# A four-row lead load and an earlier weight at the front of a bandwidth-bound channel-attention kernel

## The chip, the cores and the metric

The kernel runs on one core of one Trainium2 chip. The metric is device time in microseconds (us) for one execution. "Before" and "changed" are the two kernels. TensorE multiplies matrices, VectorE and ScalarE work element by element. SyncE and ScalarE issue the transfers, each on a queue of its own; 16 DMA engines move the packets of both queues.

## The reference

The input `x` has 1 x 384 x 384 x 384 elements in bf16 (113.25 MB), and `w1d` is a single number. The mean of every channel over all pixels, times the weight, goes through a sigmoid. Every pixel is then multiplied by that gate.

```python
g = jnp.einsum("bhwc->bc", x) / (H * W)
s = sigmoid(g * w1d[0])          # kernel size 1: no neighbours
return x * s[:, None, None, :]
```

The gate depends on all of `x`, so an honest first reading would load everything before storing anything. The kernel avoids that with a guess that it checks.

## The kernel before: the parts that matter

Each of the 128 partitions holds rows of 384 channels. There are 1152 rows per partition: one small first tile of `FIRST = 8` rows, then 26 tiles of `TILE = 44` rows in `SLOTS = 6` slots of on-chip memory (SBUF). The kernel computes an early gate, `s_early`, from only `EARLY = 4` rows of the first tile, gates and stores all tiles with it, and sums everything on TensorE on the side. At the end it computes the true gate and compares the two in bf16. Only if they differ does it run a second pass, which did not happen here.

```python
FIRST, EARLY, TILE, SLOTS, BOTH = 8, 4, 44, 6, 4
# the front: what is loaded, in which order, on which queue
load(base, FIRST, 0)                                   # SyncE: 8 rows, 128 x 6144 B
for k in range(BOTH):                                  # tiles 0..3: one half on each queue
    load(slot(k), TILE, row0(k), ("sync", "scalar"))   # 128 x 16896 B each
    if k == 0:
        plan.dma("scalar", w_one[0:1, 0:1], w1d.unsqueeze(0), writes=["w_one"])
for k in range(BOTH, SLOTS):                           # tiles 4, 5: SyncE, 128 x 33792 B
    load(slot(k), TILE, row0(k))
weight()      # TensorE broadcasts the weight, VectorE scales it
sum_first()   # TensorE sums the 4 early rows
# ... add_banks (VectorE), then s_early = sigmoid(...) on ScalarE
plan.need("tensor", ["zeros"] + rows(base, FIRST))     # TensorE waits for all 8 rows
sum_others()  # rows 4..7 of the first tile, then tile 0, 1, ...
# ... cut
for k in range(n_tiles):
    if k >= SLOTS:
        put(slot(k), TILE, row0(k - SLOTS))  # VectorE gates in place, ScalarE issues the store
        load(slot(k), TILE, row0(k))         # SyncE waits for that store, then loads
# ... cut: at the end the last six tiles and the first tile are put, then the check
ahead("sync", nc.sync, 1)     # this many transfers are issued before the start barrier
ahead("scalar", nc.scalar, 1)
```

Every store is issued on ScalarE's queue, behind that queue's own loads. VectorE gates a tile in place, so it waits until TensorE has summed that tile. TensorE works in order: the weight, the early rows, the other rows of the first tile, tile 0, and so on.

## Time and profile before

| | before |
|---|---|
| device time, median of 3 runs | 529.17 us (529.02 to 529.28) |
| span of the profiled execution | 527.6 us |
| bytes moved | 226.5 MB, half read, half written |
| TensorE busy, VectorE busy | 46%, 46% |

These are lines of the page of the kernel before. The DMA line is the busy share of the 16 DMA engines in tenths over 40 slices of 13.2 us, and the GB/s line is what they moved. The last three lines are loads: queue, number, size, and median time from issue to landing.

```profile
span 527.6 us, 1093 instructions
...
DMA  9999999999999999999999999999999999999998
GB/s 384 430 429 410 428 438 436 425 446 418 443 425 441 436 425 446 418 443 420 446 433 428 443 420 443 420 446 433 428 443 420 441 423 443 436 425 446 416 443 358
...
HBM read 113.25 MB, written 113.25 MB: 429 GB/s over the span
...
arena<-in_x_dram ACTq DMA_DIRECT2D x4, 2112.0 KB, 26.0
arena<-in_x_dram SPq DMA_DIRECT2D x4, 2112.0 KB, 30.5
arena<-in_x_dram SPq DMA_DIRECT2D x1, 768.0 KB, 7.1
```

The DMA engines are at 90% or more in every slice but the last, so the 46% of the two compute engines says that neither of them limits the time.

These are lines of the timeline of the kernel before, at its front. The columns are start, duration, engine, line, operation, count, and in brackets the idle time before it and what ended it.

```profile
12.60 0.16 PE L337 MATMUL w_all<-w_one,ones 1*128 1x1 bf16 x1 [12.60 <-DMA w_one<-in_w1d_dram]
...
16.93 0.61 ACT L369 ACTIVATE s_early<-total,w_scaled 128x384 bf16<-128x384 f32 x1 [12.55 <-DVE total L311]
17.32 8.81 PE L238 MATMUL acc<-arena,ones 128*128 128x512 bf16 x33 [1.88 <-PEq L279]
26.24 17.83 DVE L202 TENSOR_TENSOR arena<-arena,s_early 128x16896 bf16<-128x16896 bf16 x2 [9.35 <-PE acc L238]
...
35.23 0.36 ACTq L109 DMA_DIRECT2D out_dram<-arena  x1
```

The weight's matmul waited 12.60 us for the weight's landing. `s_early` was made from 16.93 us on. TensorE started on tile 0 at 17.32, VectorE on its first gate at 26.24, and the first store was issued at 35.23 us.

These are windows of the kernel before. The last two columns are the DMA share and GB/s. A packet's bytes count where it starts, so short windows wobble and the share can pass 1.

```profile
core 0: us, PE busy (x) PEld busy (x) DVE busy (x) ACT busy (x) POOL busy (x), PEclk, DMA share, GB/s
1.00:2.50 1.50, 0.00 (x0) 0.00 (x0) 0.17 (x1) 0.00 (x0) 0.06 (x2) 1.00 0.94 325
...
8.00:38.00 30.00, 19.38 (x74) 0.21 (x2) 14.51 (x10) 0.61 (x1) 0.00 (x0) 0.99 1.00 427
38.00:46.00 8.00, 7.95 (x31) 0.00 (x0) 6.07 (x1) 0.00 (x0) 0.00 (x0) 0.82 1.02 382
...
70.00:500.00 430.00, 206.33 (x712) 0.00 (x0) 188.13 (x21) 0.00 (x0) 0.00 (x0) 0.72 1.00 433
500.00:527.00 27.00, 0.62 (x3) 0.00 (x0) 14.32 (x11) 0.61 (x1) 0.00 (x0) 0.60 0.96 411
```

Between 70 and 500 us the rate is 433 GB/s. It is clearly lower in three places only: at the front, between 38 and 46 us, and at the end. To account for every tenth of a microsecond I use one derived number, the **lag**: time since the start of the span minus the bytes moved so far divided by 433.3 GB/s, with each packet's bytes of the two queues spread over its duration. At the end of the span the lag is 527.56 us minus 226.496 MB (both queues, all packets) / 433.3 GB/s = 4.84 us. At this rate, that is the most that any reordering could win.

### The profile page before, as it was taken

Reading aid. Unit: us, or ns where it says so; the run is one execution under the profiler, and the core shown is the slowest. Engines: PE = TensorE matmul, PEld = TensorE weight load, DVE = VectorE, ACT = ScalarE, POOL = GpSimd, SP = SyncE. Lnnn points to the kernel's source line nnn. Section 1 sums busy time; section 2 is a strip of 40 time slices with the busy share of each in tenths; the row PEclk is TensorE's granted clock in tenths of the full one; section 3 lists DMA queues with packets and bytes.
Section 4 is the critical chain, followed back from the end, with each engine's and each line's share of the span. In section 5 each row is a group of like instructions: output and inputs, shape, how many; then the busy total and the mean of one; then the engine's idle time right before and its main releaser. Section 6 shows DMA issues by size and latency. Waiting matters only on the chain. (4 is left out here: it accounts for less than half of the span.)

```text
span 527.6 us, 1093 instructions
## 1 busy us (share of the span) xinstructions
PE 243.7 (46%) x851; PEld 0.2 (0%) x2; DVE 241.1 (46%) x45; ACT 2.7 (1%) x4; POOL 0.3 (0%) x6
## 2 busy tenths in 40 slices
PE   0876561652651651652742642642733733633700
PEld 0000000000000000000000000000000000000000
DVE  0298626326336336336246336246156156156190
ACT  1000000000000000000000000000000000000000
POOL 0000000000000000000000000000000000000000
PEclk9998867866767867866757867868757768768765
DMA  9999999999999999999999999999999999999998
GB/s 384 430 429 410 428 438 436 425 446 418 443 425 441 436 425 446 418 443 420 446 433 428 443 420 443 420 446 433 428 443 420 441 423 443 436 425 446 416 443 358
DMA packets 8357, 226.53 MB, mean 429 GB/s; under 512 B 930, under 2 KB 930, under 8 KB 1186
## 3 DMA queue, kind: packets, MB, share of 16 engines
q10 hardware_dynamic: 4466, 121.90, 53.6%
q1 hardware_dynamic: 3888, 104.60, 46.2%
q8 instruction: 1, 0.02, 0.0%
q14 instruction: 2, 0.02, 0.0%
HBM read 113.25 MB, written 113.25 MB: 429 GB/s over the span
## 5 line engine op out<-in xcount | busy, mean ns | idle before, releaser
L238 PE MATMUL acc<-arena,ones 128*128 128x512 bf16 x846 | 242.6, 453 | 244.3 <-PEq L279 242.7
L202 DVE TENSOR_TENSOR arena<-arena,s_early 128x16896 bf16<-128x16896 bf16 (+1 forms) x27 | 234.5, 8691 | 259.2 <-PE acc L238 259.2
L337 PE MATMUL w_all<-w_one,ones 1*128 1x1 bf16 x1 | 0.2, 158 | 12.6 <-DMA w_one<-in_w1d_dram 12.6
L346 DVE TENSOR_SCALAR w_scaled<-w_all 128x1 f32<-128x1 f32 x2 | 0.2, 154 | 11.6 <-PE w_all L337 11.6
L311 DVE TENSOR_TENSOR total<-total,acc 128x128 f32<-128x128 f32 (+2 forms) x11 | 4.5, 408 | 0.3
L393 ACT ACTIVATE arena<-total,w_scaled 128x384 bf16<-128x384 f32 x1 | 0.6, 615 | 495.7 <-DVE total L311 495.7
L331 ACT ACT_TABLE_LOAD x1 | 1.3, 1283 | 2.9 <-issue 2.9
L309 DVE COPY total<-acc 128x384 f32<-128x384 f32 x1 | 0.6, 558 | 1.2 <-PE acc L238 1.2
L401 DVE TENSOR_TENSOR total<-arena,s_early 128x384 f32<-128x384 uint16 x1 | 0.6, 559 | 0.7 <-ACT arena L393 0.7
L238 PE MATMUL acc<-zeros,ones 128*128 128x512 bf16 x3 | 0.8, 380 | 0.0
L369 ACT ACTIVATE s_early<-total,w_scaled 128x384 bf16<-128x384 f32 x1 | 0.6, 615 | 12.5 <-DVE total L311 12.5
L355 DVE MEMSET ones<- 128x128 bf16 x1 | 0.2, 165 | 1.0 <-PEq L522 1.0
L236 PE MATMUL acc<-arena,ones 128*128 128x512 bf16 x1 | 0.6, 607 | 0.0
L409 DVE TENSOR_REDUCE wrong<-total 128x1 f32<-128x384 f32 x1 | 0.6, 553 | 0.0
L331 ACT ACTIVATE warm<-warm 128x1 f32<-128x1 f32 x1 | 0.2, 203 | 0.0
L415 DVE CAST redo<-wrong 128x1 int32<-128x1 f32 x1 | 0.2, 153 | 0.0
L236 PEld LDWEIGHTS acc<-arena,ones 128*128 128x128 bf16 x1 | 0.1, 106 | 0.0
L337 PEld LDWEIGHTS w_all<-w_one,ones 1*128 1x128 bf16 x1 | 0.1, 100 | 12.6 <-issue 12.6
L522 POOL MEMSET const-bfloat16-1.0<- 128x1 bf16 x1 | 0.1, 101 | 0.0
L522 POOL MEMSET const-uint8-127<- 128x1 uint8 x1 | 0.1, 101 | 0.0
L354 POOL MEMSET zeros<- 128x2 bf16 x1 | 0.1, 99 | 0.0
L353 POOL MEMSET warm<- 128x1 f32 x1 | 0.1, 98 | 0.5 <-POOLq L522 0.5
(2 smaller groups left out, 0.2 us busy)
## 6 DMA issues: line engine op xcount, KB each, us to landing
out_dram<-arena ACTq DMA_DIRECT2D x26, 4224.0 KB, 52.7
arena<-in_x_dram SPq DMA_DIRECT2D x22, 4224.0 KB, 48.1
arena<-in_x_dram ACTq DMA_DIRECT2D x4, 2112.0 KB, 26.0
arena<-in_x_dram SPq DMA_DIRECT2D x4, 2112.0 KB, 30.5
arena<-in_x_dram SPq DMA_DIRECT2D x1, 768.0 KB, 7.1
out_dram<-arena ACTq DMA_DIRECT2D x1, 768.0 KB, 16.8
w_one<-in_w1d_dram ACTq DMA_DIRECT2D x1, 0.0 KB
```

Source lines behind the costliest of these rows:

```text
L202: return lambda e: e.tensor_tensor(to_v, v, s_b, ALU.mult)
L236: loaded.append(e.matmul(bank, weights, moving, start=start, stop=stop))
L238: return e.add_instruction(mybir.InstMatmult(name=nc.get_next_instruction_name(), engine=mybir.EngineType.PE, ins=[e.lower_ap(moving), e.l ...
L309: emit = lambda e, part=part, of=of: e.tensor_copy(part, of)
L311: emit = lambda e, part=part, of=of: e.tensor_tensor(part, part, of, ALU.add)
L331: lambda e: e.activation(warm[:, 1:2], warm[:, 0:1], ACT_F.Sigmoid),
L337: lambda e: e.matmul(w_all[:, 0:1], ones[0:1, :], w_one[0:1, 0:1], start=True, stop=True),
L346: lambda e, i=i, n=n: e.tensor_scalar_mul(w_scaled[:, i : i + 1], w_all[:, 0:1], 1.0 / float(P * n)),
L369: lambda e: e.activation(s_early[:], total[:], ACT_F.Sigmoid, scale=w_scaled[:, 0:1]),
L393: lambda e: e.activation(s_true, total[:], ACT_F.Sigmoid, scale=w_scaled[:, 1:2]),
L401: lambda e: e.tensor_tensor(total[:], s_true.bitcast(U16), s_early[:].bitcast(U16), ALU.not_equal),
L409: lambda e: e.reduce_max(wrong[:], total[:], axis=mybir.AxisListType.X),
```

## The change

The intent is to get the early gate sooner. Only the 4 rows that it needs lead SyncE's queue. The weight, which stood on ScalarE's queue behind one half of tile 0 (2.2 MB), follows them directly. The other 4 rows come behind the two halves of tile 0, two rows on each queue.

```diff
-    def load(place, n, r0, queues=("sync",)):
-        i = 0
-        for queue, m in zip(queues, split(n, -(-n // len(queues)))):
+    def load(place, n, r0, queues=("sync",), lo=0, hi=None):
+        i, hi = lo, hi or n
+        for queue, m in zip(queues, split(hi - lo, -(-(hi - lo) // len(queues)))):
 ...
-    load(base, FIRST, 0)
+    load(base, FIRST, 0, hi=EARLY)
+    plan.dma("sync", w_one[0:1, 0:1], w1d.unsqueeze(0), writes=["w_one"])
     for k in range(BOTH):
         load(slot(k), TILE, row0(k), ("sync", "scalar"))
         if k == 0:
-            plan.dma("scalar", w_one[0:1, 0:1], w1d.unsqueeze(0), writes=["w_one"])
+            load(base, FIRST, 0, ("sync", "scalar"), lo=EARLY)
 ...
-    ahead("sync", nc.sync, 1)
+    ahead("sync", nc.sync, 2)
```

More of the change, by code (lines that the diff above doesn't have):

```diff
@@ L463, in ahead @@
         block[barrier:barrier] = new
-    ahead("sync", nc.sync, 1)
+    ahead("sync", nc.sync, 2)
     ahead("scalar", nc.scalar, 1)
-    plan.emit("sync", nc.sync, heads["sync"] - 1)
+    plan.emit("sync", nc.sync, heads["sync"] - 2)
     plan.emit("scalar", nc.scalar, heads["scalar"] - 1)
```

## The prediction

> **What bounds the kernel now.** The page counts 226.5 MB in a span of 527.6 us, 429 GB/s on average, and a DMA share of at least 0.9 in 39 of 40 slices; TensorE and VectorE are busy 46% each. Summing the trace's packet records in half-microsecond stretches, the 16 DMA engines run at 430 to 435 GB/s from about 8 us to 525 us. The Trainium skill ("DMA: Bandwidth & Descriptors", "Where 436 GB/s comes from") gives 435 GB/s as the ceiling of the 16 ports; the trace's 433 agrees. At 433 GB/s the bytes alone take 523.1 us. Only 4.5 us are lost: the first packet starts at 1.05 us, the engines fill by 1.75 us and run at 375 to 425 GB/s until 6 us; a dip to half rate at 40.3 to 42.6 us (about 1 us lost); and an uneven end, 525.3 to 527.1 us.
>
> **What the change does.** SyncE's first load shrinks from 128 x 6144 B to 128 x 3072 B; the other 4 rows follow behind the two halves of tile 0 as 2 x 128 packets of 1536 B; the weight leaves ScalarE's queue, where it landed at 12.5 us behind a 2.1 MB half tile, and becomes SyncE's second transfer. Bytes are unchanged, 2 DMA issues are added (0.33 to 0.5 us each by the timeline), and SyncE issues two transfers before the start barrier, which may delay the other engines by 0.4 us.
>
> **The early chain gains.** The lead load landed at 7.1 us because each DMA engine alternates by packet between the two queues (same page, "Queues, rings and completion order"; in this trace 6144 B packets take turns with 16896 B ones). I expect it at 3.5 to 4.5 us with the weight close behind; s_early, ready at 17.5 us, comes at 8 to 10 us. Tile 0's second half, landed at 17.1 us, comes at 13 to 15. Its sum on TensorE starts at about 14 instead of 17.3 us, the first gate at about 23 instead of 26.2, the first store's issue at about 32 instead of 35.2.
>
> **None of it is on the critical path.** The loads of six tiles fill the DMA engines beyond 60 us, and the first store's packets (42.6 us) stand in ScalarE's queue behind its own four half-tile loads, not behind the gate. The end (last store issued at 510.7, DMA full to 525) is untouched.
>
> **A small cost at the front.** ScalarE's first packets come at 2.46 us. Until 3.3 us the old lead load covered their slow ramp with its backlog, 0.1 to 0.15 MB. With half the bytes that backlog is gone: 0.2 to 0.3 us of DMA time lost (estimate from those records), unless ScalarE's packets come earlier. Smaller packets (0.79 MB) cost under 0.1 us more.
>
> **Predicted:** 529.3 us, range 528.5 to 530.2. Faster by over 2%: 1%; within 2%: 98%; slower by over 2%: 1%.
>
> **Checks.** Lead load and weight landing under 5 us; s_early before 11 us; first gate near 23 us; first store packet still near 42 us; DMA rate between 2 and 3.5 us lower than before; 430 to 435 GB/s from 8 to 525 us, the dip apart; span within 1 us.
>
> **What would make it wrong.** The dip near 41 us may hang on the order of transfers and vanish or double (1 us either way). The new interleaving may leave the engines less even at the end, or a queue may run dry once the stores begin: up to 1 us.

## The result, and the profile after

| | before | changed |
|---|---|---|
| device time, median of 4 runs | 529.16 us (529.02 to 529.28) | 529.04 us (528.93 to 529.18) |
| ratio | | 0.9998, 95% interval 0.9981 to 1.0015 |
| span of the profiled execution | 527.6 us | 527.5 us |

A ratio is the mean time of one kernel's fast runs over that of the other's of the same rounds, so it is not quite the ratio of the medians quoted. The verdict, at a threshold of 2%, is "same".

The page of the changed kernel, lines as shown before:

```profile
span 527.5 us, 1096 instructions
...
DMA  9999999999999999999999999999999999999998
GB/s 369 437 428 424 443 418 448 415 448 423 438 438 423 448 413 451 420 441 431 431 446 415 451 418 443 425 436 446 415 448 420 441 425 436 448 415 448 416 443 353
...
HBM read 113.25 MB, written 113.25 MB: 429 GB/s over the span
...
arena<-in_x_dram ACTq DMA_DIRECT2D x4, 2112.0 KB, 25.8
arena<-in_x_dram SPq DMA_DIRECT2D x4, 2112.0 KB, 29.6
...
arena<-in_x_dram SPq DMA_DIRECT2D x1, 384.0 KB, 3.9
arena<-in_x_dram ACTq DMA_DIRECT2D x1, 192.0 KB, 13.0
arena<-in_x_dram SPq DMA_DIRECT2D x1, 192.0 KB, 15.3
```

The lead load lands 3.9 us after its issue instead of 7.1. The trailing rows are the last two lines, and SyncE's part of them takes 15.3 us.

The timeline of the changed kernel at its front:

```profile
4.86 0.16 PE L338 MATMUL w_all<-w_one,ones 1*128 1x1 bf16 x1 [4.86 <-DMA w_one<-in_w1d_dram]
...
9.18 0.61 ACT L371 ACTIVATE s_early<-total,w_scaled 128x384 bf16<-128x384 f32 x1 [4.41 <-DVE total L312]
16.97 9.91 PE L239 MATMUL acc<-arena,ones 128*128 128x512 bf16 x36 [10.56 <-DMA arena<-in_x_dram]
27.00 17.83 DVE L202 TENSOR_TENSOR arena<-arena,s_early 128x16896 bf16<-128x16896 bf16 x2 [17.85 <-PE acc L239]
...
35.99 0.36 ACTq L109 DMA_DIRECT2D out_dram<-arena  x1
```

The weight's matmul moved from 12.60 to 4.86 us and `s_early` from 16.93 to 9.18 us: the change does what it is meant to do. But TensorE's next work starts at 16.97 us, hardly earlier than before, and the first gate at 27.00 and the first store's issue at 35.99 us are both 0.76 us *later*. The next line is from the waits of the changed kernel (total, times, longest); before, no such wait of TensorE for a load of `x` appeared.

```profile
PE acc L239 <- DMA arena<-in_x_dram: 10.6, 1, 10.6
```

The idle time of TensorE ended with a load's landing. By the landing records, tile 0's two halves landed at 11.5 and 13.6 us (12.1 and 17.1 before), and the trailing rows at 14.2 us (ScalarE's queue) and 16.9 us (SyncE's). So TensorE waited for the trailing rows. It sums them first, and tile 0 had been there for 3.3 us.

The windows of the changed kernel:

```profile
core 0: us, PE busy (x) PEld busy (x) DVE busy (x) ACT busy (x) POOL busy (x), PEclk, DMA share, GB/s
1.00:2.50 1.50, 0.00 (x0) 0.00 (x0) 0.17 (x1) 0.00 (x0) 0.13 (x2) 1.00 1.06 298
...
8.00:38.00 30.00, 17.88 (x72) 0.00 (x0) 12.08 (x5) 0.61 (x1) 0.00 (x0) 1.00 1.01 428
38.00:46.00 8.00, 7.95 (x30) 0.00 (x0) 6.83 (x1) 0.00 (x0) 0.00 (x0) 0.79 1.01 406
...
70.00:500.00 430.00, 206.40 (x714) 0.00 (x0) 190.09 (x22) 0.00 (x0) 0.00 (x0) 0.73 1.00 433
500.00:527.00 27.00, 0.00 (x0) 0.00 (x0) 12.36 (x11) 0.61 (x1) 0.00 (x0) 0.54 0.94 405
```

The front is slower (298 against 325 GB/s in the first window), the stretch from 38 to 46 us is faster (406 against 382), and the long middle is the same 433. The lag says the same in microseconds. "Switch" is the stretch from 38 to 50 us, in which ScalarE's queue goes over from loads to stores:

| lag gained in | before | changed |
|---|---|---|
| 0 to 3 us (front) | 1.61 | 1.71 |
| 3 to 38 us | 0.45 | 0.53 |
| 38 to 50 us (switch) | 1.04 | 0.58 |
| 50 to 525 us | 0.25 | 0.29 |
| 525 us to the end | 1.50 | 1.65 |
| sum | 4.84 | 4.76 |

About 0.2 us is lost up to 38 us and 0.46 us is gained at the switch. Most of the rest goes at the uneven end, where the DMA engines finish at different times. The sum agrees with the 0.07 us between the two spans. The early gate itself appears nowhere in it.

### The profile page after: what moved, and what is told of

Its sections match the earlier page's. It is cut to its first block, busy times and chain, and to the rows that moved or that the text cites. A ratio compares the mean times of both kernels' runs of the same rounds, so it can differ in the third digit from the quotient of the medians.

```text
span 527.5 us, 1096 instructions
## 1 busy us (share of the span) xinstructions
PE 243.8 (46%) x851; PEld 0.2 (0%) x2; DVE 241.1 (46%) x45; ACT 2.7 (1%) x4; POOL 0.3 (0%) x6
## 6 DMA issues: line engine op xcount, KB each, us to landing
arena<-in_x_dram SPq DMA_DIRECT2D x1, 192.0 KB, 15.3
```

## The experiments

My theory was that the DMA engines are full from the front to the end, so that the early chain (weight, `s_early`, first gate, first store's issue) can move freely within a slack. The main rival was that the early chain counts and that the gain was eaten by the trailing rows holding up TensorE. All kernels gave correct results, and every kernel was timed in up to 5 rounds beside the kernel before on the same chip. The experiments that start from the kernel before are marked so; the others start from the changed kernel.

### Trailing rows summed last: the rival's gain made real

```diff
-    add_rows(e, 1, (base + EARLY) * C, FIRST - EARLY, True, False)
+    for i in range(3): mm(e, acc[1][i][:, :], ones[:], none, True, False)   # zeros open the banks
     ... all tiles ...
-    for i in range(3): out = mm(e, acc[1][i][:, :], ones[:], none, False, True)
+    # wait for the trailing rows here, then
+    add_rows(e, 1, (base + EARLY) * C, FIRST - EARLY, False, True)
-plan.need("tensor", ["zeros"] + rows(base, FIRST))
+plan.need("tensor", ["zeros"])
```

> The changed kernel, but TensorE sums the 4 trailing rows of the first tile after all other tiles, so that their late landing (16.9 us in the changed kernel) holds up nothing. Both theories: tile 0's sum starts when its second half lands, at 13.6 to 14.2 us instead of 17.0; first gate near 23 us instead of 27.0; first store issued near 32 us instead of 36.0. Theory (the DMA engines are full from the front to the end, the early chain is off the critical path): time stays at 528.8 to 529.3 us, first store packet still near 42.5 us. Rival (the early chain counts, and the change gained nothing only because the trailing rows held up TensorE): the 4 us come off, about 525 us.

Its timeline:

```profile
14.03 9.48 PE L239 MATMUL acc<-arena,ones 128*128 128x512 bf16 x33 [6.34 <-PEq L280]
23.62 8.96 DVE L202 TENSOR_TENSOR arena<-arena,s_early 128x16896 bf16<-128x16896 bf16 x1 [14.48 <-PE acc L239]
...
32.61 0.36 ACTq L109 DMA_DIRECT2D out_dram<-arena  x1
36.43 8.96 DVE L202 TENSOR_TENSOR arena<-arena,s_early 128x16896 bf16<-128x16896 bf16 x1 [3.85 <-PE acc L239]
```

TensorE started tile 0 at 14.03 us, the first gate came at 23.62 and the first store's issue at 32.61 us, 3.4 us earlier than in the changed kernel. The median was 529.21 us (528.96 to 532.59, 6 runs) and the ratio 1.0008 (0.9993 to 1.0022). The rival's 4 us did not come off, and the first store's packet started at 42.4 us as before. So the trailing rows do explain why the first gate did not move, and moving it earlier is worth nothing. Two of the six executions, the profiled one among them, took 532.59 and 531.54 us. I come back to that under the controls.

### The weight alone (from the kernel before)

```diff
     load(base, FIRST, 0)
+    plan.dma("sync", w_one[0:1, 0:1], w1d.unsqueeze(0), writes=["w_one"])
-        if k == 0:
-            plan.dma("scalar", w_one[0:1, 0:1], w1d.unsqueeze(0), writes=["w_one"])
-    ahead("sync", nc.sync, 1)
+    ahead("sync", nc.sync, 2)
```

> The kernel before with the weight alone moved to SyncE's second transfer. Lead load lands near 7.1 us as before, weight near 7.5, s_early near 12.5 us (17.5 before); tile 0's second half still lands near 17.1, first gate still 26 to 26.5. Theory (off the path): 529.0 to 529.3 us, and the lag behind 433 GB/s at 3 us equals that of before (1.6 us), since the lead load keeps its size. Rival (the weight is what counts): faster by more than 1 us.

The lead load landed at 7.0 and the weight at 7.5 us; `s_early` was started at 11.98 us. The first gate came at 27.28 us, 0.8 us later than I expected. The median was 529.22 us (529.04 to 529.27), the ratio 1.0001 (0.9988 to 1.0014), the lag at 3 us 1.63 us, and the switch cost 0.98 us. The weight's place changes neither the front nor the switch. The rival of more than 1 us faster is out.

### The split alone

```diff
-    plan.dma("sync", w_one[0:1, 0:1], w1d.unsqueeze(0), writes=["w_one"])
         if k == 0:
+            plan.dma("scalar", w_one[0:1, 0:1], w1d.unsqueeze(0), writes=["w_one"])
             load(base, FIRST, 0, ("sync", "scalar"), lo=EARLY)
-    ahead("sync", nc.sync, 2)
+    ahead("sync", nc.sync, 1)
```

> The changed kernel with the weight back on ScalarE's queue behind its first half tile. Lead load lands near 4 us, weight near 11.5 to 12.5, s_early 16 to 17.5; trailing rows near 17, first gate 27 to 27.5. Theory: 528.9 to 529.4 us; lag behind 433 GB/s at 3 us about 1.7 us as in the changed kernel (1.61 before), so the front cost of 0.1 us belongs to the small lead load, not to the weight. Rival (the split alone is bad, the weight repays it): slower than before by 0.5 us or more.

The lead load landed at 4.2 and the trailing rows at 16.6 us; the first gate came at 26.67 us. The median was 529.11 us (528.98 to 530.5), the ratio 1.0009 (0.9996 to 1.0022). The lag at 3 us was 1.67 us, between the changed kernel's 1.71 and the 1.61 before, and the switch cost 0.77 us. Both the small loss at the front and the cheaper switch come with the split, not with the weight.

### The weight three half tiles deep: the early chain delayed on purpose

"Three deep" means that the weight stands behind three of ScalarE's half tiles; in the kernel before it stands one deep.

```diff
-    plan.dma("sync", w_one[0:1, 0:1], w1d.unsqueeze(0), writes=["w_one"])
+        if k == 2:       # after tile 2's halves
+            plan.dma("scalar", w_one[0:1, 0:1], w1d.unsqueeze(0), writes=["w_one"])
-    ahead("sync", nc.sync, 2)
+    ahead("sync", nc.sync, 1)
```

> The changed kernel made worse on purpose in its early chain: the weight stands on ScalarE's queue behind three half tiles. It should land near 32.5 us, tile 0's sum start near 35.5, first gate near 44.5, first store issued near 53.5 us: 18 us later than in the changed kernel. Theory (the loads of six tiles fill the DMA engines to about 60 us, so the chain has over 20 us of slack): time within 0.5 us, 528.6 to 529.6. Rival (the early chain is on the path, in full or in part): up to 18 us slower. Also for the dip near 41 us: if it belongs to the start of the stores, it moves to 54 to 60 us; if to ScalarE's queue running dry of loads, it stays at 41 and lasts until the stores come, and the time grows by up to 6 us.

Its timeline, then its windows from 38 us on:

```profile
33.70 0.16 PE L338 MATMUL w_all<-w_one,ones 1*128 1x1 bf16 x1 [33.70 <-DMA w_one<-in_w1d_dram]
...
38.03 0.62 ACT L372 ACTIVATE s_early<-total,w_scaled 128x384 bf16<-128x384 f32 x1 [32.84 <-DVE total L312]
45.09 17.83 DVE L202 TENSOR_TENSOR arena<-arena,s_early 128x16896 bf16<-128x16896 bf16 x2 [7.10 <-PE acc L239]
54.08 0.36 ACTq L109 DMA_DIRECT2D out_dram<-arena  x1
```

```profile
38.00:46.00 8.00, 8.00 (x36) 0.00 (x0) 0.91 (x1) 0.62 (x1) 0.00 (x0) 1.00 1.03 441
46.00:70.00 24.00, 23.84 (x110) 0.00 (x0) 24.00 (x3) 0.00 (x0) 0.00 (x0) 1.00 1.00 428
70.00:500.00 430.00, 197.62 (x699) 0.00 (x0) 210.35 (x28) 0.00 (x0) 0.00 (x0) 0.73 1.00 434
500.00:527.00 27.00, 0.00 (x0) 0.00 (x0) 2.58 (x7) 0.61 (x1) 0.00 (x0) 0.50 0.91 393
```

The first store was issued at 54.08 us, 18 us later than in the changed kernel, and the time did not move: 529.0 us median (528.62 to 529.98), ratio 1.0004 (0.9991 to 1.0017). While the gate was missing, the loads kept the engines at full rate alone: 441 GB/s in the window from 38 to 46 us. This is the strongest evidence that the early chain has slack. The slow stretch moved with the first store. The first store's packet came at 57.77 us, and in half-microsecond sums the rate was 384 to 389 GB/s from 56.5 to 57.5 us. It cost about 0.3 us between 38 and 68 us in all.

### The weight four half tiles deep: where the slack was expected to end

Same edit with `k == 3`.

> One half tile further than the run with the weight behind three halves: the weight stands behind all four of ScalarE's half tiles and lands near 43 us. First gate near 54.5 to 55.5, first store issued near 64 us. Theory (slack ends when the loads of six tiles have been read, near 60.5 us): the DMA engines stand idle from about 60.5 to about 65 us and the time grows by 4 to 5 us, to 532.5 to 534.5. If the time stays at 529, the slack is longer than I read from the records; if it grows by over 8 us, something other than that gap costs.

The first store was issued at 63.55 us. The median was 531.84 us (530.11 to 537.58, 6 runs), the ratio 1.0059 (1.0022 to 1.0097): slower, clear of the noise though far from 2%, but by less than the 4 to 5 us that I expected, and not for my reason. The last packet of the loads of six tiles ended at 64.4 us, not 60.5, because 26.7 MB at 433 GB/s take 61.7 us and the lag was 2.4 us by then. So there was a hole of only about half a microsecond near 64 us, with 190 GB/s from 64 to 64.5. From 60 to 200 us the lag grew by 2.6 us in all, most of it without idle engines: the packets themselves were longer, up to 2.6 us where 1.25 us is normal. Another 5.15 us of lag came after 525 us, at the uneven end, against 1.50 before. What makes the packets longer stays open, so this run does not show that the slack ends here: the hole alone is too small.

### The lead load late as well (from the kernel before)

```diff
-    load(base, FIRST, 0)
-        if k == 0:
+        if k == 2:
+            load(base, FIRST, 0)
             plan.dma("scalar", w_one[0:1, 0:1], w1d.unsqueeze(0), writes=["w_one"])
```

> The opposite of the change: the kernel before, with its whole 8-row lead load and the weight moved behind the third half tiles of their queues, so that the first packets on both queues have 16896 bytes and the early gate is ready only near 38 us. Theory: free, because it stays inside the slack; lag behind 433 GB/s at 3 us 1.3 to 1.5 us instead of 1.61 (before) and 1.71 (changed); the dip moves to 55 to 58 us and costs 0.2 to 0.4 us as in the run with the weight behind three halves; time 528.3 to 529.0 us. Rival (an early s_early is worth something): slower than both kernels.

This was meant to beat both kernels and did not: 529.75 us median (529.21 to 533.32, 6 runs), ratio 1.002 (0.9999 to 1.0041). The lag at 3 us was 1.87 us instead of the 1.3 to 1.5 that I expected. In its packet records the engines were busy from 1.75 us on, yet moved only 222 GB/s until 2.25 us, and ScalarE's first packet came at 2.93 instead of 2.46 us. Large packets do not shorten the ramp. The first store was issued at 59.59 us and the switch was nearly free (0.3 us between 38 and 68 us), but it gained nothing in the end.

### One row as the lead load

```diff
-    load(base, FIRST, 0, hi=EARLY)
+    load(base, FIRST, 0, hi=1)
     plan.dma("sync", w_one[0:1, 0:1], w1d.unsqueeze(0), writes=["w_one"])
+    load(base, FIRST, 0, lo=1, hi=EARLY)
```

> Doubles the suspected front cost: SyncE's lead load is one row (128 packets of 768 bytes), the other three rows of the early gate follow the weight. Theory (until ScalarE's packets come at 2.44 us the engines get only 128 packets, so their rate follows the packet size): 60 to 90 GB/s between 1.2 and 2.4 us, ScalarE's first packet still near 2.4 us, lag at 3 us 2.0 to 2.3 us (1.61 before, 1.71 changed), time 529.3 to 529.8 us. Rival (the front cost hangs on the bytes or on the number of issues, not on this wait): ScalarE's first packet comes earlier, lag stays below 1.8 us and the time at 529.1.

ScalarE's first packet came at 1.52 us, so the picture behind the theory, a fixed wait until 2.44 us, is wrong. It is not quite the rival either: the lag at 3 us rose to 1.84 us, 0.13 above the changed kernel, not 0.3 to 0.6. Lead packets of 6144, 3072 and 768 bytes thus gave 1.61, 1.71 and 1.84 us. All traces together, with their spread: 1.59 to 1.65 us with the 8-row lead load (six traces) and 1.67 to 1.74 with the 4-row one (five traces), but 1.90 in a sixth (the weight four deep), so a cost of about 0.1 us is likely and small. Five runs were 528.5 to 531.8 us, ratio 0.999 (0.9976 to 1.0005). Two more runs (540.7 and 582.1 us) are left out. This is no safe "same": the first store was issued at 41.79 us here, and the only other kernel with runs of this kind is the one with the weight two deep below (issue at 42.97 us).

### Controls: both kernels again

> The kernel before, unchanged, as a control: ratio 1.000, median within 0.15 us of the other runs of before. Its profile tells how much the dip near 41 us (about 1.0 us lost before, 0.6 in the changed kernel) varies from run to run: if this one differs from 1.0 by 0.3 us or more, the difference of the two dips is chance.

The kernel before again: 529.21 us median (529.13 to 529.4), ratio 0.9998 (0.9985 to 1.0011). Its switch cost 0.99 us, against 1.04 in the first trace.

> The changed kernel, unchanged, as a control. The variants of it that I built had single fast runs of 530 to 532.6 us, which no run of the kernel before had. If the change itself makes the time less steady, one or two of these runs are over 530 us; if it belongs to the day or to the variants, all stay between 528.8 and 529.5. Also: lag gained between 38 and 46 us (the dip) 0.5 to 0.75 us if the smaller dip (0.58 in the changed kernel, 0.67 and 0.76 in two variants with the split, 0.97 to 1.04 in three traces without it) belongs to the split; near 1.0 if it was chance.

The changed kernel again: 529.09 us median (528.88 to 531.11), ratio 1.0006 (0.9995 to 1.0018). The profiled execution was the one of 531.11 us. Its switch cost 0.55 us, against 0.58 in the first trace. So the difference of the switch is not chance: four traces with the 8-row lead load and the first store issued before 38 us have 0.98 to 1.05 us (before, its control, the weight alone, and the last experiment below), and the four with the split and such an early first store have 0.55 to 0.77 (changed, its control, trailing rows last, the split alone). Why the split makes it cheaper is not settled.

In the 531.11 us execution, 77 of SyncE's whole-tile packets between 66 and 500 us took over 1.27 us, and in the 532.59 us one of the trailing-rows-last kernel 93 did. In the first traces of before and changed none did. The busy share there was full, so those packets were slow, not late. All 51 executions of the kernel before, its control included, stayed at or below 529.68 us, and one of 9 of the changed kernel was above 530. That hints that the changed order is a little less steady. One in nine does not prove it. Counted afterwards over all kernels with a first store issued before 38 us, it is 4 of 20 executions above 530 us with the split (changed, trailing rows last, the split alone) and none of 61 without it (before, the weight alone, the gate held back). That is a stronger hint, but no test that was planned.

### The weight two and three half tiles deep, lead load unsplit (from the kernel before)

```diff
-        if k == 0:
+        if k == 1:       # two deep;  k == 2 for three deep
             plan.dma("scalar", w_one[0:1, 0:1], w1d.unsqueeze(0), writes=["w_one"])
```

> The kernel before with the weight two half tiles deep on ScalarE's queue instead of one: lands near 23 us, first gate near 35, first store issued near 44.5 us, when ScalarE's queue has read all its loads (last one ends near 42.8). The opposite direction of the change and nothing else. Theory: inside the slack, and without the small lead load: lag at 3 us 1.6 us. If the dip is small when ScalarE's queue is dry before the first store (0.07 to 0.25 us in the runs with late stores, against 0.6 to 1.0), the time is 528.3 to 528.8; if the small dip of those runs had another reason, 529.1 as before. Rival (an early gate is worth something): slower than before.

> The same one half tile deeper: weight near 33 us, first store issued near 54 us, still 10 us before the loads of six tiles end at 64 us. Theory: as the run with the weight two deep, 528.3 to 528.9 us, dip moved to 56 to 58 us and 0.2 us deep. Rival: slower than before, and slower than two deep.

Three deep (first store issued at 53.04 us): 529.25 us median (529.12 to 530.69), ratio 1.0009 (0.9996 to 1.0021). The slack holds, but the gain that I hoped for did not come. The cheaper switch (0.5 us from 38 to 68 us, against 1.04 before) was given back later: 0.46 us from 68 to 525 us and 1.89 us at the end, against 0.25 and 1.50 before.

Two deep (first store issued at 42.97 us) was the surprise: four runs of 530.36, 531.14, 537.60 and 537.75 us, ratio 1.0096 (1.005 to 1.0143), and two runs besides (539.77 and 580.43 us). With one core there is no second die to compare, so these two were told apart by their time alone (over 1.5% above the kernel's fastest); 539.77 us may be of the same kind as 537.75 us. Both my expectation of 528.3 to 528.8 us and that of a small dip fell; the switch cost 0.61 us. The windows of its profiled execution, the one of 531.14 us:

```profile
38.00:46.00 8.00, 8.00 (x38) 0.00 (x0) 8.00 (x2) 0.00 (x0) 0.00 (x0) 1.00 1.03 435
46.00:70.00 24.00, 15.01 (x60) 0.00 (x0) 23.55 (x3) 0.00 (x0) 0.00 (x0) 0.79 1.01 427
70.00:500.00 430.00, 204.02 (x714) 0.00 (x0) 191.43 (x22) 0.00 (x0) 0.00 (x0) 0.72 1.00 433
500.00:527.00 27.00, 0.00 (x0) 0.00 (x0) 11.01 (x11) 0.61 (x1) 0.00 (x0) 0.54 0.93 402
```

The engines are full at 433 GB/s here too, and the loss shows as long packets and an uneven end (3.3 us of lag after 525 us, against 1.5 before). A store issued 11 us later than this one costs nothing, so missing slack is not the likely reason. But this kernel, with its first store 7.7 us later than the kernel before, did cost time, and that limits the theory. The executions of 537 us were not profiled.

### The gate held back on VectorE (from the kernel before)

```diff
     # after s_early
+    for _ in range(27):
+        plan.op("vector", lambda e: e.tensor_copy(total[:], total[:]), reads=["total"], writes=["total"])
```

> The kernel before with 27 in-place copies (0.56 us each by its profile) on VectorE after s_early, so that the first gate starts near 33.5 us and the first store is issued near 42.5 us, as in the run with the weight two deep (42.97 us), while the weight, the loads and TensorE's early sums stay as before. It settles what made that run slow (530.4 to 537.8 us in fast runs) though the dependencies leave slack: if the moment of the first store, with ScalarE's queue run dry, decides, this run is slow and uneven too (over 530 us in most executions); if it was the weight's place or TensorE's delay, this run is 529.0 to 529.4 us. In both cases no idle DMA time between 2 and 525 us; a loss shows as longer packets.

The dose was too small. A copy took 0.39 us, not the 0.56 us of the copy from another memory that I had scaled from:

```profile
17.73 10.63 DVE L378 COPY total<-total 128x384 f32<-128x384 f32 x27 [0.68 <-ACT s_early L369]
...
28.27 17.82 DVE L202 TENSOR_TENSOR arena<-arena,s_early 128x16896 bf16<-128x16896 bf16 x2
37.26 0.36 ACTq L109 DMA_DIRECT2D out_dram<-arena  x1
```

The first store was issued at 37.26 us instead of 35.23, not at 42.5. The time stayed at 529.2 us median (528.93 to 529.5), ratio 0.9998 (0.9985 to 1.0012). The question of the two-deep run stays open. One thing it does show: the slow stretch began near 40.5 us and the first store's packet came at 42.7 us, as before, though the issue was 2 us later. With the stores queued behind loads (issued from 32.61 to 37.26 us in these traces), it is the end of those loads on ScalarE's queue, not the store's issue, that sets when the switch comes.

## Why the prediction was right, and where it was not

- **The time**: predicted 529.3 us, range 528.5 to 530.2; measured 529.04 us. Shown: the early chain made 3.4 us faster than in the changed kernel, or 18 us slower, leaves the medians at 529.21 and 529.0 us. That the time came so close to the kernel before is in part luck: the loss at the front (0.2 us by 38 us) and a gain at the switch (0.46 us) that I had only named as a risk nearly cancelled. And slack in any amount is not shown: in the kernel with its first store 7.7 us later (two deep) the fast runs took 530.4 to 537.8 us.
- **"The lead load at 3.5 to 4.5 us with the weight close behind; s_early at 8 to 10 us"**: right. It landed at 3.9, the weight at 4.7, and `s_early` was started at 9.18 us.
- **"Its sum on TensorE starts at about 14, the first gate at about 23, the first store's issue at about 32"**: wrong. TensorE started at 16.97 us, and with the trailing rows; the first gate and the first store's issue came at 27.00 and 35.99 us. The failed step is that I let tile 0's sum start when tile 0's second half is there (predicted 13 to 15 us, measured 13.6) and gave no landing time for the trailing rows, for which TensorE waits first. The Trainium skill says that a DMA engine takes turns between queues by the packet ("DMA: Bandwidth & Descriptors", "Queues, rings and completion order"), and I had used that for the lead load, but not here. SyncE's 128 trailing packets of 1536 bytes stood behind tile 0's half and took turns with ScalarE's own trailing packets until 13.78 us and with its 16896 byte packets of tile 1. They needed 12.85 to 15.86 us for 0.2 MB and landed at 16.91. With these rows summed last, the three steps came at 14.03, 23.62 and 32.61 us, as predicted.
- **"The first store's packets stand behind ScalarE's own loads"**: right. They start at 42.57 us (42.59 before), and at 42.4 us with the issue 3.4 us earlier.
- **"A small cost at the front, 0.2 to 0.3 us"**: right in direction, too large for the front alone. It was 0.10 us by 3 us, and 0.18 by 38 us with the small packets. The mechanism that I gave, a backlog that covers ScalarE's slow ramp, is not what the records show: the loss is already there before ScalarE's first packet at 2.44 us (lag 1.68 against 1.59 us). From 1.8 to 2.2 us the 3072 byte packets moved 246 to 266 GB/s, the 6144 byte ones before 371 to 381. Packet size alone is not shown as the cause: 16896 byte packets moved 223 GB/s there (the lead load late).
- **"The dip may hang on the order of transfers"**: named as a risk, and it does. It fell from about 1.0 to 0.6 us in every trace with the split, which repays the front's loss.

Left open: why the split makes the switch cheaper; why packets run long in some executions and above all with the weight two deep; and whether the changed kernel is less steady. No version that I ran beats both kernels.

## What to carry to other kernels

When the DMA engines are full from the first microseconds to the last, count the lag behind the full rate stretch by stretch before you shorten any chain: a chain that ends inside the time which queued loads cover can often move by many microseconds for nothing. Test each position all the same: the two kernels here with a first store 18 us later lost nothing that shows, the one with it 7.7 us later did, for a reason that stays open. Small transfers placed behind large ones on two shared queues can land late, by the number of packets and not by their bytes (3.0 us for 0.2 MB here), so do not let an in-order engine wait for them first. Time a reordering over several executions, not one: a kernel here that differs from the one before only in where a 2 byte transfer stands spread from 530 to 538 us.

## What the Trainium skill lacked or had wrong

- "DMA: Bandwidth & Descriptors", "Where 436 GB/s comes from", says that for transfers between HBM and SBUF a per-core limit of about 358 GB/s binds, and also that its own large transfer ran near the fabric's 435. Here one core sustained 433 GB/s from 70 to 500 us with loads and stores mixed, so the 358 did not bind. The sentence lacks the condition that the same page gives above it: each core gets about 358 GB/s when both cores of the HBM domain stream. This program ran on one core. That the 435 is what bound was not tested; the 433 is close to it.
- The same page, "Latency and other measured facts", gives about 0.6 us to the first byte of such a queue. SyncE's first packet came 1.05 us after its issue began and 0.67 after the issue ended, which fits. Nothing there says that a second queue starts later: ScalarE's first packet came 1.95 us after its issue ended (at 2.46 us), at 1.52 us with a one-row lead load and at 2.93 us with large packets on both queues.
- The same page, "Queues, rings and completion order", speaks of packets of about 9 to 17 descriptors. What these records call a packet is one partition's row: 128 for each of these loads, 1536 to 33792 bytes. Whether that is the page's packet or a part of it, no run here shows. While SyncE's 128 rows of 1536 bytes passed (12.85 to 15.86 us), 88 such rows and 61 of 16896 bytes passed on ScalarE's queue.
- No page has the slow stretch before a first store: with loads in flight, the rate fell to 220 to 237 GB/s from 41 to 42.5 us in the kernel before and to 291 at the lowest in the changed one, and was back above 425 by 44 us with the stores flowing (0.55 to 1.05 us lost in the eight traces with a first store issued before 38 us).
